# Grouped-query attention decode: K rows of 8 KB in 1 MB loads, two pairs of groups interleaved by halves of the keys

## The chip, the cores and the metric

The kernel runs on one core of one Trainium2 chip. The metric is device time in microseconds (us) of one execution. A core has the matrix engine PE (its weight loads are listed apart, as PEld), the vector engine DVE, the scalar engine ACT, GpSimd (POOL), the queue SP, which in this kernel only issues DMA transfers, and 16 DMA engines that carry them.

## The reference, cut to what matters

```python
B, Hq, Hkv, Sq, Sk, D = 16, 32, 8, 16, 2048, 128      # all bfloat16
k = jnp.repeat(k, Hq // Hkv, axis=1)                  # 4 query heads share one K/V head
v = jnp.repeat(v, Hq // Hkv, axis=1)
scores = jnp.einsum("bhqd,bhkd->bhqk", q, k) * D ** -0.5
p = softmax(scores, axis=-1)
return jnp.einsum("bhqk,bhkd->bhqd", p, v)
```

One group is one (batch, K/V head): 128 groups, each with 64 query rows (4 heads of 16) against 2048 keys. K and V are 512 KB a group, so 134.2 MB of K and V are read once and 4.2 MB of Q and output go beside them.

## The kernel before, in words

Groups are worked in 64 pairs p, the two groups of a pair filling the 128 rows of a tile. For each pair, in the names of the code:

- K: a DMA of 512 KB for each group g into the ring `Kn` (NBK = 10 buffers). Partition a gets the 16 consecutive keys 16a to 16a+15, so each partition receives 4 KB in one piece.
- kx: DVE transposes the tile in 32x32 blocks of 32-bit words into `KT` (L267; NKT = 3 buffers of a pair).
- S: 32 matmuls write the scores into `S_ps` (L340), which fills four PSUM banks and exists once. Each of the four banks holds the keys of 32 partitions of K (a in the code).
- ex: ACT takes the exponential of all 2048 columns in one instruction, into `P` (2 buffers), with the row sums by the accumulator (L278). No maximum is subtracted in this fast program; a second, general program, which does, stands behind a branch at the end and is taken only if a row sum leaves a range.
- pt, pe: 16 PE transposes in two halves into `PT_ps` (L350), each half copied by DVE or ACT to `PT` (L299; NPT = 3).
- V, pv: a DMA of 512 KB for each group into `Vb` (NBV = 14), and 32 matmuls into `O_ps` (L355).
- rc, nm, ST: the reciprocal of the row sum (L284), the scaled copy to `O` (L288 on ACT, L290 on DVE; NBO = 8), and the store of 32 KB.

Q comes in 8 chunks of 256 KB (8 pairs each); POOL rearranges it (qr, L272), PE transposes it (qt, L328) and ACT or DVE copies it out (qe, L299).

Every transfer is issued by SP at L317, in one written order (`dma` in `make_ops`): at step t the two K loads of pair t, the two V loads of pair t - DV (DV = 2) and the store of pair t - DSTORE (DSTORE = 5). SP waits for each transfer's condition before it issues it, so a store that waits for its nm holds back all loads behind it. The order of the work on the other engines is fixed when the kernel is built: `build_schedule` runs a small model of the engines with the durations in `_DUR`, and each engine then follows its list, with semaphore waits taken from `deps`. `HINT` places, for each engine, a mark so many operations ahead of the end for the branch there.

The code that the diff touches follows.

Of the kernel before, what the change touches and what calls it, by code (L numbers as in the profile page):

```python
# [12 lines left out]
NBK = 10  # L13
NBV = 14
# [3 lines left out]
DV = 2  # L18
# [4 lines left out]
HINT = {"pe": 7, "dve": 10, "act": 3, "pool": 1, "sp": 6}  # L23
# [4 lines left out]
    ("dve", "kx"): 1.25, ("dve", "mx"): 2.38, ("dve", "rc"): 0.17, ("dve", "nm"): 0.36,  # L28
    ("dve", "pe"): 0.69, ("act", "pe"): 1.03, ("act", "qe"): 1.06, ("dve", "qe"): 1.25, ("act", "nm"): 0.42,
    ("act", "ex"): 2.22, ("pool", "qr"): 1.6, ("act", "qr"): 1.1, ("dve", "qr"): 1.1,  # L30
# [6 lines left out]
_SIZE = {"K": 0.524, "V": 0.524, "Q": 0.27, "ST": 0.06}  # L37
_ISSUE = 0.5
_T0 = 1.0
_ENGS = {"kx": ("dve",), "mx": ("dve",), "rc": ("dve",), "nm": ("act", "dve"), "pe": ("act", "dve"),  # L40
         "qe": ("act", "dve"), "qr": ("pool",), "ex": ("act",), "qt": ("pe",), "S": ("pe",), "pt": ("pe",), "pv": ("pe",)}
_PRIO = {"S": 0, "mx": 0, "ex": 0, "pt": 1, "pe": 1, "pv": 2, "rc": 2, "nm": 2, "kx": 3, "qr": 3, "qt": 3, "qe": 3}


def make_ops(NP, pairs_per_chunk, general):

    deps = {}
    dma = []
    ch = lambda p: p // pairs_per_chunk
    n_ch = ch(NP - 1) + 1  # L50
    last_of = lambda c: min(NP, (c + 1) * pairs_per_chunk) - 1

    def add(op, *d):
        deps[op] = [x for x in d if x is not None]

    opt = lambda ok, op: op if ok else None
    for c in range(n_ch):
        add(("Q", c), *[opt(c >= 2, ("qr", c - 2, x)) for x in range(4)])
        for x in range(4):
            prev = ("qe", c, x - 1) if x else opt(c >= 1, ("qe", c - 1, 3))  # L60
            add(("qr", c, x), ("Q", c), opt(c >= 1, ("qt", c - 1, x)))
            add(("qt", c, x), ("qr", c, x), prev)
            add(("qe", c, x), ("qt", c, x), opt(c >= 2, ("S", last_of(c - 2))))
    for g in range(2 * NP):
        p = g // 2
        add(("K", g), opt(g >= NBK, ("kx", g - NBK)))
        add(("V", g), opt(g >= NBV, ("pv", (g - NBV) // 2)))
        add(("kx", g), ("K", g), opt(p >= NKT, ("S", p - NKT)))
    for p in range(NP):
        add(("S", p), ("kx", 2 * p), ("kx", 2 * p + 1), *[("qe", ch(p), x) for x in range(4)],  # L70
            opt(p >= 1, ("mx" if general else "ex", p - 1)))
        if general:
            add(("mx", p), ("S", p), opt(p >= 2, ("ex", p - 2)))
        add(("ex", p), ("mx" if general else "S", p), *[opt(p >= 2, ("pt", p - 2, h)) for h in range(2)])
        for h in range(2):
            add(("pt", p, h), ("ex", p), opt(p >= 1, ("pe", p - 1, h)))
            add(("pe", p, h), ("pt", p, h), opt(p >= NPT, ("pv", p - NPT)))
        add(("pv", p), ("pe", p, 0), ("pe", p, 1), ("V", 2 * p), ("V", 2 * p + 1), opt(p >= 1, ("nm", p - 1)))
        add(("rc", p), ("ex", p))
        add(("nm", p), ("pv", p), ("rc", p), opt(p >= NBO, ("ST", p - NBO)))  # L80
        add(("ST", p), ("nm", p))
    qstep = {max(0, c * pairs_per_chunk - QLEAD): c for c in range(n_ch)}
    dma.append(("Q", 0))
    for t in range(NP + max(DV, DSTORE) + 1):
        if t < NP:
            dma += [("K", 2 * t), ("K", 2 * t + 1)]
        if qstep.get(t, 0):
            dma.append(("Q", qstep[t]))
        if 0 <= t - DV < NP:
            dma += [("V", 2 * (t - DV)), ("V", 2 * (t - DV) + 1)]  # L90
        if 0 <= t - DSTORE < NP:
            dma.append(("ST", t - DSTORE))
    return deps, dma


def pair_of(op, pairs_per_chunk):
    if op[0] in ("qr", "qt", "qe"):
        return op[1] * pairs_per_chunk - 1.5
    return op[1] // 2 if op[0] == "kx" else op[1] + {"S": -1.5, "pv": 1.5}.get(op[0], 0)


def build_schedule(NP, pairs_per_chunk, general):

    deps, dma = make_ops(NP, pairs_per_chunk, general)
    left = sorted((op for op in deps if op[0] in _ENGS),
                  key=lambda op: (pair_of(op, pairs_per_chunk), _PRIO[op[0]]))
    done, free = {}, {"pe": _T0, "dve": _T0, "act": _T0, "pool": _T0, "sp": _T0}
    progs = {"pe": [], "dve": [], "act": [], "pool": [], "sp": []}
    dma_left, dma_end = list(dma), _T0 + _DMA_LAT

    def ready(op):
        r = 0.0
        for d in deps[op]:
            if d not in done:
                return None
            r = max(r, done[d])
        return r

    while left or dma_left:
        best = None  # L120
        if dma_left:
            rd = ready(dma_left[0])
            if rd is not None:
                st = max(free["sp"] + _LAT_SAME, rd + _LAT)
                best = ((round(st, 3), -1, -1), st, "sp", dma_left[0])
        seen = 0
        for op in left:
            rd = ready(op)
            if rd is None:
                continue  # L130
            dur = lambda e: _DUR[op[0]] if e == "pe" else _DUR[(e, op[0])]
            engs = ("dve", "act") if op[:2] == ("qr", 0) else _ENGS[op[0]]
            fin = min((max(free[e] + _LAT_SAME, rd + _LAT) + dur(e), e) for e in engs)
            st = fin[0] - dur(fin[1])
            cand = ((round(st, 3), pair_of(op, pairs_per_chunk), _PRIO[op[0]]), st, fin[1], op)
            if best is None or cand[0] < best[0]:
                best = cand
            seen += 1
            if seen > 40:
                break  # L140
        _, st, eng, op = best
        if eng == "sp":
            dma_left.pop(0)
            end = st + _ISSUE
            dma_end = max(dma_end, end + _DMA_LAT) + _SIZE[op[0]] / _BW
            done[op] = dma_end + (_V_LATE if op[0] == "V" else 0.0)
        else:
            left.remove(op)
            end = st + (_DUR[op[0]] if eng == "pe" else _DUR[(eng, op[0])])
            done[op] = end  # L150
        free[eng] = end
        progs[eng].append(op)
    return deps, progs, max(done.values())


def bass_standalone__gqa_softmax__sampling_kernel(
# [28 lines left out]
    Kn = [sb(f"Kn{i}", [128, J * 64], I32) for i in range(NBK)]  # L185
    KT = [sb(f"KT{i}", [128, 2, J * 64], I32) for i in range(NKT)]
    Vb = [sb(f"Vb{i}", [128, J, 128], BF16) for i in range(NBV)]
    Sneg = [sb(f"Sneg{i}", [128, Sk], F32) for i in range(2)]
# [3 lines left out]
    nbias = sb("nbias", [128, NP], F32)  # L192
    rowsum = sb("rowsum", [128, NP], F32)
    ones = sb("ones", [128, 1], F32)
# [13 lines left out]
    rings = {"K": NBK, "V": NBV, "Q": 2, "ST": NBO}  # L208

    class Program:  # L210
        def __init__(self, tag, general):
            self.general = general
            self.deps, self.progs, _ = build_schedule(NP, qch // 128, general)
            self.sem_eng = {e: sem(f"{tag}_{e}") for e in ("pe", "dve", "act", "pool")}
            self.sem_dma = {kind: [sem(f"{tag}_{kind}{i}") for i in range(n)] for kind, n in rings.items()}
            self.where = {op: (e, i + 1) for e in self.sem_eng for i, op in enumerate(self.progs[e])}

        def point(self, op):
            if op[0] in rings:
                n = rings[op[0]]  # L220
                return self.sem_dma[op[0]][op[1] % n], 16 * (op[1] // n + 1)
# [36 lines left out]
    def elementwise(eng, me, prog, before_last=None):  # L258
        waits = prog.waiter(eng, me)
        for op in prog.progs[me]:  # L260
# [5 lines left out]
            if kind == "kx":  # L266
                ins = eng.transpose(KT[(p // 2) % NKT][:, p % 2, :], Kn[p % NBK][:, :])  # L267
# [5 lines left out]
            elif kind == "mx":  # L273
                ins = eng.tensor_scalar(Sneg[p % 2][:, :], S_ps[:, :], -scale, None,
                                        op0=ALU.mult, op1=ALU.min, accum_out=nbias[:, p:p + 1])
            elif kind == "ex":
                src = Sneg[p % 2] if prog.general else S_ps
                ins = eng.activation(  # L278
                    P[p % 2][:, :].rearrange("m (r a j) -> m a r j", a=4, j=32),
                    src[:, :].rearrange("m (a r j) -> m a r j", a=4, j=32), ACT.Exp,  # L280
                    bias=nbias[:, p:p + 1] if prog.general else 0.0, scale=-1.0 if prog.general else scale,
                    accum_out=rowsum[:, p:p + 1])
# [19 lines left out]
    def transfers(sp, prog):  # L302
        waits = prog.waiter(sp, "sp")
        for op in prog.progs["sp"]:
# [3 lines left out]
            s = x % rings[kind]  # L308
            if kind == "K":
                dst, src = Kn[s][:, :].bitcast(BF16), kf[x].rearrange("(a j) d -> a (j d)", j=J)  # L310
            elif kind == "V":
                dst, src = Vb[s][:, :, :], vf[x].rearrange("(a j) d -> a j d", j=J)
# [6 lines left out]
    def matmuls(pe, prog):  # L319
        waits = prog.waiter(pe, "pe")  # L320
        for op in prog.progs["pe"]:
# [11 lines left out]
            elif kind == "S":  # L333
                c, pp = divmod(p, qch // 128)
                for x in range(4):
                    for a in range(4):
                        for gg in range(2):
# [14 lines left out]
            else:  # L352
                for r in range(J):
                    for gg in range(2):
# [3 lines left out]
                            Vb[(2 * p + gg) % NBV][:, r, :],  # L358
# [20 lines left out]
    with nc.Block() as block:  # L379
# [30 lines left out]
        def _(dve):  # L410
            def count_within():
                dve.wait_ge(*fast.point(("ex", NP - 1)))
# [41 lines left out]
```

## Time and profile before

| what | value |
|---|---|
| median of 3 runs | 356.95 us (356.61 to 357.4) |
| the profiled execution, its own time | 355.28 us |
| its span, first to last instruction | 353.4 us |
| granted TensorE clock, mean | 0.971 |
| DMA, share of the span and mean rate | 98.7% of 16 engines, 394 GB/s |
| DVE, PE, ACT busy | 239.4, 233.8, 193.8 us |
| landing of a K load, of a V load (median from issue) | 12.1 us, 13.3 us |

The profile describes one execution. Busy time is given for each engine and as a share of the span; idle time before a group of instructions is put down to whatever released it last. The DMA queues are listed by packets, bytes and the time that the packets took as a share of 16 engines' time; packets on one engine can overlap, so a share may read a little over 100%. Row 2 of the page cuts the span into 40 slices of 8.8 us.

### The profile page before, as it was taken

Reading aid. Unit: us, or ns where it says so; the run is one execution under the profiler, and the core shown is the slowest. Engines: PE = TensorE matmul, PEld = TensorE weight load, DVE = VectorE, ACT = ScalarE, POOL = GpSimd, SP = SyncE. Lnnn points to the kernel's source line nnn. Section 1 sums busy time; section 2 is a strip of 40 time slices with the busy share of each in tenths; the row PEclk is TensorE's granted clock in tenths of the full one; section 3 lists DMA queues with packets and bytes.
Section 4 is the critical chain, followed back from the end, with each engine's and each line's share of the span. In section 5 each row is a group of like instructions: output and inputs, shape, how many; then the busy total and the mean of one; then the engine's idle time right before and its main releaser. Section 6 shows DMA issues by size and latency. Waiting matters only on the chain.

```text
span 353.4 us, 11937 instructions
## 1 busy us (share of the span) xinstructions
PE 233.8 (66%) x5378; PEld 167.9 (48%) x5378; DVE 239.4 (68%) x340; ACT 193.8 (55%) x214; POOL 28.9 (8%) x35
## 2 busy tenths in 40 slices
PE   2499765776666857756556876676656677566663
PEld 1266543554444634544444655454444545444442
DVE  4668786787685666766766676675776647866761
ACT  6458555754347646665456753576554755554450
POOL 1040000300012000310004000040000400000000
PEclk9999999989999998999999988999999989999997
DMA  7999999999999999999999999999999999999971
GB/s 276 414 408 408 413 408 407 412 413 406 413 408 410 412 410 412 408 413 411 410 411 411 408 412 413 395 411 413 409 411 409 406 413 410 403 409 405 411 287 42
DMA packets 47288, 139.24 MB, mean 394 GB/s; under 512 B 13440, under 2 KB 13440, under 8 KB 47232
## 3 DMA queue, kind: packets, MB, share of 16 engines
q1 hardware_dynamic: 47232, 138.43, 98.7%
q8 instruction: 43, 0.70, 0.8%
q14 instruction: 13, 0.11, 0.1%
HBM read 136.31 MB, written 2.10 MB: 392 GB/s over the span
## 4 chain that ended last, share of the span: by engine, by line
DMA 54%; PE 16%; DVE 14%; ACT 7%; SPq 5%; issue 4%
DMA Kn<-in_k_dram 54%; DVE KT L267 8%; ACT P L278 6%; PE S_ps L340 6%; SPq L317 5%; PE PT_ps L350 5%; PE O_ps L355 5%; DVE PT L299 4%; DVE O L290 1%; PE QT_ps L328 1%; ACT O L288 0%; DVE rrec L284 0%; DVE flag L419 0%
## 5 line engine op out<-in xcount | busy, mean ns | idle before, releaser
L267 DVE STREAM_TRANSPOSE KT<-Kn 128x1024 int32<-128x1024 int32 x128 | 158.1, 1238 | 75.7 <-DMA Kn<-in_k_dram 74.6
L278 ACT ACTIVATE P<-S_ps 128x2048 bf16<-128x2048 f32 x64 | 120.1, 1877 | 78.0 <-PE S_ps L340 77.8
L350 PE MATMUL PT_ps<-ident,P 128*128 128x128 bf16 x1024 | 76.0, 225 | 53.9 <-DVE PT L299 38.3
L340 PE MATMUL S_ps<-KT,QT 32*64 32x512 bf16 x2048 | 74.6, 398 | 45.8 <-DVE KT L267 16.8
L350 PEld LDWEIGHTS PT_ps<-ident,P 128*128 128x128 bf16 x1024 | 60.4, 100 | 77.8 <-issue 40.9
L299 DVE COPY PT<-PT_ps 128x1024 bf16<-128x1024 bf16 x102 | 66.1, 672 | 16.7 <-PE PT_ps L350 16.7
L355 PE MATMUL O_ps<-Vb,PT 128*64 128x128 bf16 x2048 | 73.1, 225 | 6.5 <-issue 5.4
L355 PEld LDWEIGHTS O_ps<-Vb,PT 128*64 128x64 bf16 x2048 | 61.8, 113 | 21.2 <-issue 16.9
L340 PEld LDWEIGHTS S_ps<-KT,QT 32*64 32x64 bf16 x2048 | 28.9, 105 | 69.0 <-DVE KT L267 34.3
L272 POOL COPY Qr<-Qn 128x1024 bf16<-128x1024 bf16 x28 | 27.9, 1041 | 250.4 <-DMA Qn<-in_q_dram 250.4
L288 ACT ACTIVATE O<-O_ps,rrec 128x128 bf16<-128x128 f32 x27 | 9.9, 367 | 56.7 <-PE O_ps L355 56.7
L299 ACT ACTIVATE QT<-QT_ps 128x1024 bf16<-128x1024 bf16 x30 | 30.6, 1019 | 6.6 <-PE QT_ps L328 6.6
L299 ACT ACTIVATE PT<-PT_ps 128x1024 bf16<-128x1024 bf16 x26 | 26.6, 1024 | 5.7 <-PE PT_ps L350 5.7
L328 PE MATMUL QT_ps<-ident,Qr 128*128 128x128 bf16 x256 | 22.4, 238 | 8.4 <-ACT Qr L272 4.5
L328 PEld LDWEIGHTS QT_ps<-ident,Qr 128*128 128x128 bf16 x256 | 17.4, 107 | 12.2 <-issue 7.4
L290 DVE TENSOR_SCALAR O<-O_ps,rrec 128x128 bf16<-128x128 f32 x37 | 12.7, 342 | 7.6 <-PE O_ps L355 7.2
L284 DVE RECIPROCAL rrec<-rowsum 128x1 f32<-128x1 f32 x64 | 9.5, 149 | 4.7 <-ACT P L278 3.8
L278 ACT ACTIVATION_READ_ACCUMULATOR P<-S_ps 128x1 f32 x64 | 12.4, 194 | 0.0
L272 DVE COPY Qr<-Qn 128x1024 bf16<-128x1024 bf16 x2 | 1.3, 690 | 3.3 <-DMA Qn<-in_q_dram 3.3
L299 DVE COPY QT<-QT_ps 128x1024 bf16<-128x1024 bf16 x2 | 2.5, 1225 | 1.2 <-PE QT_ps L328 1.1
L272 ACT ACTIVATE Qr<-Qn 128x1024 bf16<-128x1024 bf16 x2 | 2.0, 1049 | 1.3 <-DMA Qn<-in_q_dram 1.3
L272 ACT ACT_TABLE_LOAD x1 | 1.3, 1283 | 0.7 <-PEq L439 0.7
(12 smaller groups left out, 2.2 us busy)
## 6 DMA issues: line engine op xcount, KB each, us to landing
Kn<-in_k_dram SPq DMA_DIRECT2D x128, 512.0 KB, 12.1
Vb<-in_v_dram SPq DMA_DIRECT2D x128, 512.0 KB, 13.3
Qn<-in_q_dram SPq DMA_DIRECT2D x8, 256.0 KB, 12.0
out_dram<-O SPq DMA_DIRECT2D x64, 32.0 KB, 11.0
```

What stands on the lines that cost most here:

```text
L267: ins = eng.transpose(KT[(p // 2) % NKT][:, p % 2, :], Kn[p % NBK][:, :])
L272: ins = eng.activation(dst, src, ACT.Copy) if me == "act" else eng.tensor_copy(dst, src)
L278: ins = eng.activation(P[p % 2][:, :].rearrange("m (r a j) -> m a r j", a=4, j=32), src[:, :].rearrange("m (a r j) -> m a r j", a=4, j=32) ...
L284: ins = eng.reciprocal(rrec[:, p:p + 1], rowsum[:, p:p + 1])
L288: ins = eng.activation(dst, src, ACT.Copy, scale=r)
L290: ins = eng.tensor_scalar(dst, src, r, None, op0=ALU.mult)
L299: ins = eng.activation(dst, src, ACT.Copy) if me == "act" else eng.tensor_copy(dst, src)
L317: sp.dma_start(dst, src).then_inc(prog.sem_dma[kind][s], 16)
L328: ins = pe.transpose(QT_ps[:, 128 * i:128 * (i + 1)], Qr[:, x, i, :], ident[:, :],)
L340: ins = pe.matmul(S_ps[64 * gg:64 * (gg + 1), 512 * a:512 * (a + 1)], QT[c % 2][32 * a:32 * (a + 1), x, 128 * pp + 64 * gg:128 * pp + 64 * ...
L350: ins = pe.transpose(PT_ps[h][:, 128 * t:128 * (t + 1)], P[p % 2][:, 128 * r:128 * (r + 1)], ident[:, :])
L355: ins = pe.matmul(O_ps[64 * gg:64 * (gg + 1), 0:128], PT[p % NPT][:, r, 64 * gg:64 * (gg + 1)], Vb[(2 * p + gg) % NBV][:, r, :], start=(r ...
```

## The change

- K: four groups (two pairs, p = 2s and 2s+1) share the partitions. Load i = 2s + gg is 1 MB and brings group gg of both pairs: 64 partitions hold one group, 64 the other, each partition 32 consecutive keys, 8 KB in one piece. `Kn` has 6 buffers of 1 MB. On the DRAM side the transfer now counts 2 groups, 64 rows, 8 KB; on the side of the chip's memory 128 partitions.
- S: a step u = 2s + h covers one half of the keys (16 of each partition's 32) of both pairs, so `S_ps` holds 1024 columns of either pair. The transposes kx stay as many and as large.
- ex: two instructions of 1024 columns for each pair, with their row sums in `rhalf`, which a new operation rs on DVE adds.
- V: still 512 KB a transfer and 4 KB a partition, but partition 64h + b takes keys 32b + 16h to 32b + 16h + 15, to match K; on the DRAM side the transfer counts 2 halves, 64 rows, 4 KB. The last pair's V comes in two parts (VH), and its pv is cut in two likewise.
- The written order of the transfers: V runs LAG = 5 pairs behind K in place of 2, the store 5 pairs behind V. `Vb` has 7 buffers of a pair (as much memory as before).
- `HINT` is 200, 10000 and 130 for DVE, ACT and SP, and the planner's durations follow the new shapes. In the general program the negated scores use two of the `Kn` buffers.

```diff
-NBK = 10
-NBV = 14
+NBK = 6
+NBK_GENERAL = 4
+NBV = 7
...
-DV = 2
+LAG = 5
...
-HINT = {"pe": 7, "dve": 10, "act": 3, "pool": 1, "sp": 6}
+HINT = {"pe": 7, "dve": 200, "act": 10000, "pool": 1, "sp": 130}
...
-    ("act", "ex"): 2.22, ("pool", "qr"): 1.6, ("act", "qr"): 1.1, ("dve", "qr"): 1.1,
+    ("act", "nm"): 0.42, ("act", "ex"): 1.27, ("pool", "qr"): 1.6, ("act", "qr"): 1.1, ("dve", "qr"): 1.1,
...
+    v_of = lambda p: [("VH", x) for x in halves] if p == NP - 1 else [("V", p)]
...
+    for i in range(NP):
+        add(("K", i), *[opt(i >= nbk, ("kx", 2 * ((i - nbk) // 2) + h, i % 2)) for h in halves])
...
+    for u in range(NP):
+        s, h = divmod(u, 2)
+        for gg in range(2):
+            add(("kx", u, gg), ("K", 2 * s + gg), opt(u >= NKT, ("S", u - NKT)))
+        prev = [("mx" if general else "ex", 2 * ((u - 1) // 2) + pp, (u - 1) % 2) for pp in range(2)] if u else []
+        add(("S", u), ("kx", u, 0), ("kx", u, 1), *[("qe", ch(2 * s), x) for x in range(4)], *prev)
...
+            add(("ex", p, h), ("nb", p) if general else ("S", u), *[opt(p >= 2, ("pt", p - 2, x)) for x in halves])
...
+            add(("pt", p, h), ("ex", p, 0), ("ex", p, 1), opt(p >= 1, ("pe", p - 1, h)))
+            add(("pe", p, h), ("pt", p, h), opt(p >= NPT, ("pv", p - NPT, 0)))
...
+        add(("rs", p), ("ex", p, 0), ("ex", p, 1))
...
-    for t in range(NP + max(DV, DSTORE) + 1):
+    lag = min(LAG, nbk - 1)
+    for t in range(NP + max(lag, DSTORE) + 1):
         if t < NP:
-            dma += [("K", 2 * t), ("K", 2 * t + 1)]
+            dma.append(("K", t))
...
+        if 0 <= t - lag < NP:
+            dma += v_of(t - lag)
+        if 0 <= t - lag - DSTORE < NP:
+            dma.append(("ST", t - lag - DSTORE))
...
-                ins = eng.transpose(KT[(p // 2) % NKT][:, p % 2, :], Kn[p % NBK][:, :])
+                gg, i = op[2], 2 * (p // 2) + op[2]
+                ins = eng.transpose(KT[p % NKT][:, gg, :],
+                                    Kn[i % prog.rings["K"]][:, J * 64 * (p % 2):J * 64 * (p % 2 + 1)])
...
+                    src = S_ps[:, Sk // 2 * (p % 2):Sk // 2 * (p % 2 + 1)]
                 ins = eng.activation(
-                    P[p % 2][:, :].rearrange("m (r a j) -> m a r j", a=4, j=32),
-                    src[:, :].rearrange("m (a r j) -> m a r j", a=4, j=32), ACT.Exp,
+                    P[p % 2][:, :].rearrange("m (r h a j) -> m h a r j", h=2, a=2, j=32)[:, h],
+                    src.rearrange("m (a r j) -> m a r j", a=2, j=32), ACT.Exp,
...
             if kind == "K":
-                dst, src = Kn[s][:, :].bitcast(BF16), kf[x].rearrange("(a j) d -> a (j d)", j=J)
-            elif kind == "V":
-                dst, src = Vb[s][:, :, :], vf[x].rearrange("(a j) d -> a j d", j=J)
+                dst = Kn[s][:, :].bitcast(BF16)
+                src = kf[4 * (x // 2) + x % 2:4 * (x // 2) + x % 2 + 3:2].rearrange("p (b r) d -> p b (r d)", r=2 * J)
+            elif kind[0] == "V":
+                p, part = (x, slice(0, J)) if kind == "V" else (NP - 1, slice(J // 2 * x, J // 2 * (x + 1)))
+                for gg in range(2):
+                    sp.dma_start(
+                        Vb[p % NBV][:, gg, part, :].rearrange("a r d -> a (r d)"),
+                        vf[2 * p + gg].rearrange("(b h r) d -> h b r d", h=2, r=J)[:, :, part, :]
+                        .rearrange("h b r d -> h b (r d)"),
+                    ).then_inc(prog.sem_dma[kind][s], 16)
+                continue
...
                     for a in range(4):
+                        c, pp = divmod(2 * (p // 2) + a // 2, qch // 128)
```

## The prediction

> **What bounds the kernel now.** I read the page first: the shares of the engines, the 40 slices, the DMA queues.
>
> ```profile
> PE 233.8 (66%) x5378; PEld 167.9 (48%) x5378; DVE 239.4 (68%) x340; ACT 193.8 (55%) x214; POOL 28.9 (8%) x35
> ...
> DMA  7999999999999999999999999999999999999971
> GB/s 276 414 408 408 413 408 407 412 413 406 413 408 410 412 410 412 408 413 411 410 411 411 408 412 413 395 411 413 409 411 409 406 413 410 403 409 405 411 287 42
> DMA packets 47288, 139.24 MB, mean 394 GB/s; under 512 B 13440, under 2 KB 13440, under 8 KB 47232
> ...
> q1 hardware_dynamic: 47232, 138.43, 98.7%
> ```
>
> No compute engine passes 68%, while the DMA engines are full in 37 slices of 40 at 395 to 414 GB/s. The kernel is a stream of 139 MB with a short head and a tail. The longest wait, POOL for Q, costs nothing: POOL has 29 us of work.
>
> Two views tell whether compute could become the limit. In the groups by line:
>
> ```profile
> L267 DVE STREAM_TRANSPOSE KT<-Kn 128x1024 int32<-128x1024 int32 x128 | 158.1, 1238 | 75.7 <-DMA Kn<-in_k_dram 74.6
> L278 ACT ACTIVATE P<-S_ps 128x2048 bf16<-128x2048 f32 x64 | 120.1, 1877 | 78.0 <-PE S_ps L340 77.8
> ```
>
> DVE, the busiest engine, waits 74.6 us for K itself: compute keeps up and is paced by the loads. The chain of waits says the same (54% of it is K's loads).
>
> Last the end: windows of the DMA and the timeline.
>
> ```profile
> 338.00:340.00 2.00, 0.82 (x36) 0.61 (x38) 1.75 (x4) 1.54 (x2) 0.00 (x0) 1.00 0.92 364
> 340.00:341.00 1.00, 1.00 (x37) 0.46 (x22) 0.16 (x1) 0.11 (x1) 0.00 (x0) 1.00 0.79 311
> 341.00:345.00 4.00, 2.89 (x63) 2.45 (x60) 2.74 (x5) 1.86 (x2) 0.00 (x0) 1.00 0.54 212
> 345.00:346.00 1.00, 0.46 (x17) 0.49 (x19) 0.35 (x1) 0.00 (x0) 0.00 (x0) 1.00 0.31 104
> ...
> 345.51 0.95 PEld L355 LDWEIGHTS O_ps<-Vb,PT 128*64 128x64 bf16 x32 [0.67 <-issue]
> 345.54 1.08 PE L355 MATMUL O_ps<-Vb,PT 128*64 128x128 bf16 x32 [0.54 <-DVE O L290]
> ...
> 347.16 1.08 PE L355 MATMUL O_ps<-Vb,PT 128*64 128x128 bf16 x32 [0.54 <-DVE O L290]
> ...
> 348.28 0.35 DVE L290 TENSOR_SCALAR O<-O_ps,rrec 128x128 bf16<-128x128 f32 x1 [0.99 <-PE O_ps L355]
> ```
>
> The last two columns of the windows are DMA share and GB/s. From 341 to 345 half the engines' time is used at half the rate: I read it as half of the engines having finished some 4 to 5 us before the rest. The last V has landed by about 345.7. The last two pv then wait for the nm before them (DVE O), so a compute chain ends the kernel: last scaled copy done at 348.63, store, 353.4.
>
> **The change part by part.** I sum against the profiled execution: span 353.4, its own time 355.28. The median of runs, 356.95, lies 1.67 above that; I add it at the end.
>
> K's packets. K has 128 loads of 128 rows of 4 KB, 16384 packets; after, 64 loads of 128 rows of 8 KB, 8192. Of the 13440 short packets 64 x 128 = 8192 are output rows of 256 B; the other 5248 are 16 for each of 328 transfers, its completion marks. After there are 64 K, 130 V, 8 Q and 64 store transfers, 266 x 16 = 4256 marks. VH adds 256 packets of 2 KB. So 8192 + 992 - 256 = 8928 packets fewer, 558 for each engine. Fixed cost of a packet: no less than 0, if time goes by bytes. Upper end from the last store alone (window 348.5 to 351.2):
>
> ```profile
> q1 hardware_dynamic: 144, 0.03, 5.6%
> ```
>
> 5.6% of 16 x 2.7 us is 2.42 us; 144 packets hold 128 x 256 B, 1.28 us at 25.7 B/ns (411 GB/s over 16); 1.14 us / 144 = 8 ns. The gain lies between 0 and 558 x 8 ns = 4.5 us. A 4 KB load is neither end, so I take 4 ns: -2.2 us, all on the path, as the stream is full.
>
> [...]
>
> The end. With V 5 pairs behind K, the last K lands some 6 MB before the last V, 15 us at 411 GB/s. Its transposes, S, exponentials and PE transposes took from 335.08 to 344.9 before, 10 us, so they lie under V's loads. What is left behind the last V: half a pv (16 matmuls, 0.55 us by 1.08 for 32), nm 0.35 with 0.15 of handoffs, and the way from 348.63 to 353.4, 4.8 us: 5.9 us, against 353.4 - 345.7 = 7.7 now: -1.8. Bounds: -2.5, if V's landing is half a microsecond later than I read; 0, if the last pv still queues behind earlier ones.
>
> The dips. Slices of 395, 403, 403 and 405 cost 38/411 x 8.8 = 0.8 us. SP's queue waits 126 us for nm to send stores (64.8 ACT O, 61.3 DVE O), and loads stand behind. After, with V 5 behind and the store 5 behind V, five V and five K of 1 MB are out when SP waits, 25 us of work against a landing of 12 to 13 now. A stall of nm (7.1 us at most) is covered: -0.5 (bounds 0 and -0.8). Without that cover each microsecond that SP waits beyond the queue's content is lost.
>
> What beside the stream gets longer. ACT: 128 exponentials of 1024 columns. The nearest rows are copies of 128x1024, 1019 to 1024 ns, plus 194 to read the accumulator: 1.22 us. Bounds of the instruction: 0.94, half of 1877, and 1.88, no gain from halving. 128 x 1.22 = 156 against 64 x 2.07 = 132.5: +23 us, ACT 217 (62%). DVE: 64 additions at most like the reciprocal, 149 ns: +9.5, DVE 249 (71%); behind each wait only reciprocal and nm, due 10 us later. Kx, S, pt and pv keep number and size. These hide under 5.3 us a pair (139.24 MB / 64 / 411).
>
> The loop to watch is `S_ps`, which exists once. Now S to next S is 3.3 us (exponentials at 337.57 and 340.89 with one S between). After, a half-step of two pairs is S 1.13, two exponentials 2.44, handoffs 0.13: two half-steps 7.4 us for two pairs, for which the stream needs 10.6. The rest of ACT's work, 193.8 - 132.5 = 61 us, adds 1.9 for two pairs if none of it lies under S: 9.3. Covered, with 1.3 to spare.
>
> V's rows are as many and as long but 8 KB apart in turn; the trace has only V read in order. No gain; at worst all V runs at the poorest slice, 395 against 411: 4% of 170 us, +7. I take 0, as the two halves together read the same contiguous 512 KB. The head: the first S stood at 13.3 behind Q's copies, and 2 MB of K had landed by 11: 0 (to +1). `HINT`: its effect lies in the 4.8 us at the end; 0, bounds -1 and +2.
>
> Sum: -2.2 - 1.8 - 0.5 = -4.5. Span 348.9, own time 350.8, as a median 352.4.
>
> **The rivals.** (a) Nothing measurable (within 0.2%, 0.7 us, what a measurement can tell from no change): rows of 8 KB cost per byte what 4 KB does, and the last pv still queues behind pv(62). The half-idle DMA from 341 to 345 speaks for a limit that packet size doesn't touch; the DVE O waits speak against. 356.95 less at most 0.7: 356.6.
>
> (b) Slower, the ring of `S_ps`: it decides once two half-steps pass 10.6 us, that is when an exponential with its accumulator costs over (10.6 - 2.26 - 0.26 - 1.9) / 4 = 1.55 us. At the upper bound, 1.88 + 0.19, two pairs take 12.7 us, 32 x 12.7 + 13 + 10 = 429; slightly over the point, 11 us: 375. The copies of 128x1024 at 1020 ns speak against, and DVE could take more of ACT's copies.
>
> (c) Slower, a transfer that is spread over fewer engines. All transfers now count 128 rows outermost on both sides, and the 16 marks for each show all 16 engines. K and V after count 2 outermost in DRAM. If that count sets the spread, 134.2 MB go over two engines of 25.7 GB/s: 2610 us, and the marks of a load fall from 16 to 2. No row shows a transfer with a small outer count, for or against; an even spread by the 128 partitions would give the forecast.
>
> [...]
>
> (d) Slower by V's interleaved reads: 1 to 2% over, 357.7 to 362.
>
> **How the numbers follow.** Forecast 0.66 (it takes in the packet gain or the shorter end failing alone: 354.7, 354.2), (a) 0.07, (b) 0.08, (c) 0.12, (d) 0.07. Low end: all bounds at their best, -4.5 - 2.5 - 0.8 - 1 = -8.8: 348.2; I take 347.5. High end: into (d), 359.5; (b), (c) and a rest of (d) stay out, near 0.2. The forecast's own range is 348 to 356. Faster by over 0.2%: 0.66; within: 0.07; slower: 0.27.
>
> **What would show it.** q1 with some 38300 packets, 12450 of them under 512 B; slices at 412 to 416 and none under 408; ACT near 217, DVE near 249; exponentials of about 1020 ns; the chain's end on V's landing, with 16 matmuls, nm and store behind; the last kx over 10 us ahead of it. It is wrong if slices stay at 410, if DVE or ACT stop waiting for loads, or if the DMA share falls to an eighth.

## The result and the profile after

The changed kernel takes 2561.8 us (2561.5 to 2562.1, 4 runs) against 357.2 us before: 7.174 times as long, 95% interval 7.162 to 7.186. The forecast was 352.4 us with a range of 347.5 to 359.5; the time lies near rival (c), a transfer spread over fewer engines, which had been priced at 2610 us and given 0.12.

The profiled execution took 2562.1 us, with a span of 2560.2. The page of the changed kernel, shares of the engines, granted clock, slices and queues:

```profile
PE 377.4 (15%) x5378; PEld 266.8 (10%) x5378; DVE 225.2 (9%) x365; ACT 230.7 (9%) x381; POOL 29.0 (1%) x35
...
PEclk9755555555555555555555555555555555555555
DMA  1111111111111111111111111111111111111111
GB/s 58 53 53 53 53 57 54 54 54 54 58 54 54 54 54 57 54 54 54 54 57 54 54 54 54 57 54 53 54 54 58 54 54 54 54 54 54 54 54 53
DMA packets 35642, 139.21 MB, mean 54 GB/s; under 512 B 9732, under 2 KB 9732, under 8 KB 27396
...
q1 hardware_dynamic: 35588, 138.42, 13.3%
```

In all 40 slices, now of 64 us, the DMA engines are busy for about one eighth of their time and move 53 to 58 GB/s, where it had been 395 to 414. The bytes are the same 138.4 MB. 13.3% of 16 engines is 2.1 engines: two that never rest, and a little on the others. The packet records of the trace (start, length and size of every packet) say so directly: at least two packets are under way in 99.7% of the span, three or more in 4.6%. A 4 KB packet takes 159 ns (median) in both kernels. So the two engines are no slower than before; there are only two of them.

The short packets say which transfers use so few engines. 9732 packets are under 512 B; 8192 of them are output rows. The other 1540 are completion marks: 16 for each of the 8 Q loads and 64 stores make 1152, and 388 remain for the 64 K loads and 130 V loads, exactly 2 each. Before there were 16 for every transfer.

The waits of the changed kernel, the longest first (us in total, times, longest):

```profile
DVE KT L287 <- DMA Kn<-in_k_dram: 2210.5, 64, 37.5
POOL Qr L293 <- DMA Qn<-in_q_dram: 1933.3, 7, 316.1
ACT O L318 <- PE O_ps L394: 1154.6, 47, 36.2
PEld O_ps L394 <- DMA Vb<-in_v_dram: 1043.9, 64, 35.2
```

DVE waited 74.6 us for K before, now 2210.5. No compute engine is the limit: each is idle for five sixths of the span or more. SP's queue in the timeline (start, duration, number of transfers):

```profile
1000.38 8.02 SPq L355 DMA_DIRECT2D Kn<-in_k_dram  x1
...
1008.45 27.90 SPq L345 DMA_DIRECT2D Vb<-in_v_dram  x2
```

To hand over two V loads takes SP 27.9 us, where the median of one was 0.48 us. What holds SP in that time is not shown.

Two groups of the page belong to steps of the prediction:

```profile
L306 ACT ACTIVATE P<-S_ps 128x1024 bf16<-128x1024 f32 x128 | 130.4, 1021 | 699.2 <-PE S_ps L378 658.8
...
L378 PE MATMUL S_ps<-KT,QT 32*64 32x512 bf16 x2048 | 115.4, 588 | 529.9 <-DVE rowsum L312 306.2
```

The halved exponential takes 1021 ns (estimate 1.02 us). A score matmul averages 588 ns where it was 398; the mean granted clock fell with it, from 0.971 to 0.546 of full speed.

### The profile page after: what moved, and what is told of

It is laid out like the page before. It is cut to its first block, busy times and chain, and to the rows that moved or that the text cites. A ratio compares the mean times of both kernels' runs of the same rounds, so it can differ in the third digit from the quotient of the medians.

```text
span 2560.2 us, 12003 instructions
## 1 busy us (share of the span) xinstructions
PE 377.4 (15%) x5378; PEld 266.8 (10%) x5378; DVE 225.2 (9%) x365; ACT 230.7 (9%) x381; POOL 29.0 (1%) x35
## 2 busy tenths in 40 slices
DMA packets 35642, 139.21 MB, mean 54 GB/s; under 512 B 9732, under 2 KB 9732, under 8 KB 27396
## 3 DMA queue, kind: packets, MB, share of 16 engines
q1 hardware_dynamic: 35588, 138.42, 13.3%
## 4 chain that ended last, share of the span: by engine, by line
DMA 55%; SPq 37%; PE 3%; DVE 3%; issue 1%; ACT 1%; another core or an unknown queue 1%; POOL 0%
DMA Kn<-in_k_dram 50%; SPq L345 23%; SPq L355 13%; DMA Vb<-in_v_dram 4%; DVE KT L287 2%; PE S_ps L378 2%; DMA Qn<-in_q_dram 1%; PE PT_ps L388 1%; DVE PT L329 0%; ACT P L306 0%; PE QT_ps L366 0%; PE O_ps L394 0%; DVE QT L329 0%; ACT PT L329 0%
## 5 line engine op out<-in xcount | busy, mean ns | idle before, releaser
L287 DVE STREAM_TRANSPOSE KT<-Kn 128x1024 int32<-128x1024 int32 x128 | 154.4, 1229 | 2210.5 <-DMA Kn<-in_k_dram 2210.5
L394 PE MATMUL O_ps<-Vb,PT 128*64 128x128 bf16 x2048 | 122.9, 314 | 1032.4 <-DMA Vb<-in_v_dram 1032.4
L394 PEld LDWEIGHTS O_ps<-Vb,PT 128*64 128x64 bf16 x2048 | 107.3, 172 | 1052.6 <-DMA Vb<-in_v_dram 1043.9
L388 PE MATMUL PT_ps<-ident,P 128*128 128x128 bf16 x1024 | 116.6, 303 | 535.1 <-DVE PT L329 512.8
L378 PE MATMUL S_ps<-KT,QT 32*64 32x512 bf16 x2048 | 115.4, 588 | 529.9 <-DVE rowsum L312 306.2
L306 ACT ACTIVATE P<-S_ps 128x1024 bf16<-128x1024 f32 x128 | 130.4, 1021 | 699.2 <-PE S_ps L378 658.8
L388 PEld LDWEIGHTS PT_ps<-ident,P 128*128 128x128 bf16 x1024 | 101.0, 141 | 575.1 <-issue 475.6
L329 ACT ACTIVATE PT<-PT_ps 128x1024 bf16<-128x1024 bf16 x50 | 50.8, 1016 | 140.5 <-PE O_ps L394 103.2
L329 DVE COPY PT<-PT_ps 128x1024 bf16<-128x1024 bf16 x78 | 50.6, 662 | 1.3 <-PE PT_ps L388 1.3
L329 ACT ACTIVATE QT<-QT_ps 128x1024 bf16<-128x1024 bf16 x25 | 25.5, 1021 | 270.4 <-PE QT_ps L366 270.4
L293 POOL COPY Qr<-Qn 128x1024 bf16<-128x1024 bf16 x28 | 27.9, 1040 | 1933.3 <-DMA Qn<-in_q_dram 1933.3
L306 ACT ACTIVATION_READ_ACCUMULATOR P<-S_ps 128x1 f32 x128 | 25.2, 197 | 0.0
L312 DVE TENSOR_TENSOR rowsum<-rhalf 128x1 f32<-128x1 f32 x64 | 9.0, 171 | 1.9 <-ACT P L306 1.9
```

The source lines that it names most:

```text
L287: ins = eng.transpose(KT[p % NKT][:, gg, :], Kn[i % prog.rings["K"]][:, J * 64 * (p % 2):J * 64 * (p % 2 + 1)])
L293: ins = eng.activation(dst, src, ACT.Copy) if me == "act" else eng.tensor_copy(dst, src)
L306: ins = eng.activation(P[p % 2][:, :].rearrange("m (r h a j) -> m h a r j", h=2, a=2, j=32)[:, h], src.rearrange("m (a r j) -> m a r j", a ...
L312: ins = eng.tensor_tensor(rowsum[:, p:p + 1], rhalf[:, p, 0:1], rhalf[:, p, 1:2], op=ALU.add)
L329: ins = eng.activation(dst, src, ACT.Copy) if me == "act" else eng.tensor_copy(dst, src)
L378: ins = pe.matmul(S_ps[64 * gg:64 * (gg + 1), 512 * a:512 * (a + 1)], QT[c % 2][32 * a:32 * (a + 1), x, 128 * pp + 64 * gg:128 * pp + 64 * ...
```

## The experiments

The time of before in the three groups of runs was 356.47 us (e1 to e4), 356.02 (e5 to e8) and 356.16 (e9 to e12); each run is compared with its own.

**e1_outer4: an outermost count of 4, and nothing else.**

```diff
-                dst, src = Kn[s][:, :].bitcast(BF16), kf[x].rearrange("(a j) d -> a (j d)", j=J)
+                dst, src = Kn[s][:, :].bitcast(BF16), kf[x].rearrange("(b c j) d -> c b (j d)", c=4, j=J)
...
-                dst, src = Vb[s][:, :, :], vf[x].rearrange("(a j) d -> a j d", j=J)
+                dst = Vb[s][:, :, :].rearrange("a j d -> a (j d)")
+                src = vf[x].rearrange("(b c j) d -> c b (j d)", c=4, j=J)
```

> The kernel before, with one edit: the rows of K and of V are dealt to the partitions in 4 blocks, so that every K and V load counts 4 outermost in DRAM (4 blocks, 32 rows, 4 KB) against 128 partitions. Bytes, transfers, order and computation are those of before. Theory (the outermost count sets how many engines carry a load): in the changed kernel two engines moved 134.7 MB (all K and V, an eighth of Q and stores) in 2558 us, 26.3 GB/s each; four engines then need 135.2 MB / 105.3 GB/s = 1284 us, so 1290 us in all, with 256 x 4 + 72 x 16 = 2176 completion marks and 10368 packets under 512 B. Rival (the loss lies in the dealt rows or in loads of 1 MB, and all 16 engines are used): under 450 us here, with 13440 short packets as before.

Measured: 1308.0 us. The queues of its page:

```profile
DMA packets 44215, 139.22 MB, mean 107 GB/s; under 512 B 10368, under 2 KB 10368, under 8 KB 44160
...
q1 hardware_dynamic: 44160, 138.42, 26.4%
```

10368 short packets, to the packet; 26.4% of 16 engines is 4.2 engines. The time is 1.4% over the expectation. By the packet records at least four packets are under way in 98.8% of the span, five or more in 11.6%. A count of 4 gave four engines, in the kernel before with its 512 KB loads and 4 KB rows.

**e9_before_outer2: the same edit with c=2.**

> The kernel before, with K's and V's rows dealt to the partitions in 2 blocks, so that each load counts 2 outermost in DRAM; nothing else of the change (no 8 KB rows, no 1 MB loads, no halves, no lag). Theory: this alone gives the changed kernel's time: 134.7 MB over two engines of 26.3 GB/s, 2560 us, within 1% of 2562; 8192 + 256 x 2 + 72 x 16 = 9856 short packets. Rival (half of the changed kernel's loss comes from its other parts): under 2300.

Measured: 2583.4 us, 0.8% over the changed kernel.

```profile
DMA packets 43704, 139.23 MB, mean 54 GB/s; under 512 B 9856, under 2 KB 9856, under 8 KB 43648
...
q1 hardware_dynamic: 43648, 138.42, 13.3%
```

9856 short packets, as worked out. This one edit of the source patterns alone gives the whole of the changed kernel's loss; the changed kernel, with its fewer and longer rows, is 22 us shorter than this one.

**e3_k_in_halves: K alone mended** (the semaphore counts, left out here, follow).

```diff
-                dst = Kn[s][:, :].bitcast(BF16)
-                src = kf[4 * (x // 2) + x % 2:4 * (x // 2) + x % 2 + 3:2].rearrange("p (b r) d -> p b (r d)", r=2 * J)
+                for y in range(2):
+                    sp.dma_start(
+                        Kn[s][64 * y:64 * (y + 1), :].bitcast(BF16),
+                        kf[4 * (x // 2) + x % 2 + 2 * y].rearrange("(b r) d -> b (r d)", r=2 * J),
+                    ).then_inc(prog.sem_dma[kind][s], 16)
+                continue
```

> The changed kernel, each K load of 1 MB issued as two of 512 KB, one for each half of the partitions (64 rows of 8 KB outermost on both sides, same addresses). V is left as it is. Theory: K now uses all 16 engines, V stays on two, which carry 67.1 MB of V, an eighth of K (8.4 MB) and of the rest (0.5 MB): 76.0 MB / 52.7 GB/s = 1443 us. Rival (loads of 8 KB rows or the deep queue are slow whatever the engines): above 1900 us.

Measured: 1664.2 us, 15% over the theory's number and under the rival's. Between its first slice and its last three the rate swings between 71 and 97 GB/s. SP waits 332 us for exponentials, but the two engines of V hardly stood still for it: by the packet records at least two packets are under way in 99.4% of the span. The sum went wrong in the packets' length. An 8 KB packet of K takes 607 ns on average, where it took 311 in the changed kernel, and a 4 KB packet 183 in place of 160; an estimate from these times is some 150 us more for K's share on each engine and 180 for V's, enough for the 221 us over the sum. The next runs show the same of loads into half of the partitions.

**e4_all_in_halves: K and V mended in the same way** (V as four loads of 64 rows for a pair).

> The changed kernel with both K and V issued by halves of the partitions (K two loads of 512 KB, V four of 256 KB for a pair; 64 rows outermost on both sides). Addresses, layout, order and computation are those of the changed kernel. Theory: all loads on 16 engines, 8192 + 16 x (128 + 260 + 72) = 15552 short packets, and the forecast's own sum applies but for the marks, which now are more than before and not fewer: 351 to 355 us. Rival (the S_ps ring or the lag of 5 is a second cause): 360 us and up, with ACT or DVE no longer waiting for loads.

Measured: 550 to 563 us in six runs, 1.552 times before (1.546 to 1.557). The theory's number failed, and the rival's reason as well: ACT and DVE have 228 and 224 us of work, and DVE waits 297 us for K. The DMA is full and slow:

```profile
DMA  8999999999999999999999999999999999999992
GB/s 195 215 225 224 231 238 255 275 258 264 279 271 257 269 272 252 263 270 259 268 251 256 257 267 254 250 259 265 267 260 247 260 261 253 254 264 271 274 268 75
DMA packets 41464, 139.25 MB, mean 251 GB/s; under 512 B 15552, under 2 KB 15552, under 8 KB 33216
```

All marks are there (15552 short packets), so all 16 engines work, at 251 GB/s on average. Their packets take longer: 264 ns (median) for 4 KB in place of 159, 527 for 8 KB in place of 309. So 16 engines alone did not give the rate of before, 394 GB/s on average.

**e7_before_halves and e8_before_columns: the kernel before, each load cut in two**, by partitions and by columns (V's lines and the semaphore counts are left out here).

```diff
-                dst, src = Kn[s][:, :].bitcast(BF16), kf[x].rearrange("(a j) d -> a (j d)", j=J)
+                for y in range(2):                                       # e7; V likewise
+                    sp.dma_start(Kn[s][64 * y:64 * (y + 1), :].bitcast(BF16),
+                                 kf[x].rearrange("(a j) d -> a (j d)", j=J)[64 * y:64 * (y + 1), :]).then_inc(prog.sem_dma[kind][s], 16)
+                for y in range(2):                                       # e8; V likewise
+                    sp.dma_start(Kn[s][:, 512 * y:512 * (y + 1)].bitcast(BF16),
+                                 kf[x].rearrange("(a j) d -> a (j d)", j=J)[:, 1024 * y:1024 * (y + 1)]).then_inc(prog.sem_dma[kind][s], 16)
```

> The kernel before, each K and V load of 512 KB issued as two of 256 KB, one for partitions 0 to 63, one for 64 to 127; rows of 4 KB, natural order, all else as before. Theory (a transfer into half of the partitions does not reach the full rate, although 64 rows divide over 16 engines): the 251 GB/s of e4_all_in_halves, 139.2 MB / 251 = 555 us; 480 to 580. Rival (e4 lost its time to V's rows read 8 KB apart, or to the S_ps ring): 358 to 370 here, as nothing but the number of transfers differs from before.

> The kernel before, each K and V load of 512 KB issued as two of 256 KB over all 128 partitions, 2 KB of each partition's row: as many transfers and as large as in e7_before_halves, but each reaches every partition. Theory of half partitions: no such loss; 2304 packets more an engine at 4 ns are 9 us: 357 to 376. Rival (smaller transfers are what costs): as slow as e7.

Measured: e7 476.3 us, e8 373.7 us. The same number of transfers of the same size; only the one that reaches half of the partitions loses its rate. The slices of e7:

```profile
GB/s 204 234 231 234 244 244 249 249 247 253 248 251 250 248 241 258 266 282 315 290 357 376 387 285 352 393 392 302 326 359 347 315 286 344 369 375 367 362 341 70
```

The rate stays at 204 to 258 for 16 slices of 40, then climbs, and swings up to 393. So the same transfers run slowly first and near the full rate later; what changes between is not shown. e8 is 17.7 us over before with 2304 packets more for an engine: 7.7 ns each.

**e2_outer16: 16 engines, rows dealt in 16 blocks** (the edit of e1 with c=16).

> The same edit with 16 blocks of 8 rows: neighbouring partitions read rows 64 KB apart from each other in turn, and the outermost count is 16. Theory: all 16 engines, 13440 short packets, and the time of before within 1% (355 to 361). Rival (the dealt rows themselves are slow to read): clearly slower than before, 380 us and up, as no dealing goes further than this one.

Measured: 445.8 us in the fastest of four runs (the others 454 to 495), with all 13440 short packets. That is 1.25 times before, so the theory's second half failed: with 16 engines the time of before does not return. The number fits the rival, slow reading of dealt rows, as well; e10 and e11 test that. The slices begin as in e7:

```profile
GB/s 201 239 235 239 244 249 252 253 259 280 306 334 383 297 386 386 376 320 318 359 375 389 279 395 387 366 289 306 368 376 371 254 358 390 342 343 367 362 274 35
```

**e10_k_columns and e11_k_outer16: which of the two, far reads or the outermost count.** Both start from e5_adjacent_groups below and load K in two transfers of 512 KB (the semaphore counts are left out here).

```diff
-                src = kf[2 * x:2 * x + 2].rearrange("g (b r) d -> (g b) (r d)", r=2 * J)
+                for y in range(2):       # e10; e11 reads "g (e y w r) d -> y (g e) w (r d)", y=2, w=8
+                    sp.dma_start(Kn[s][:, J * 64 * y:J * 64 * (y + 1)].bitcast(BF16),
+                                 kf[2 * x:2 * x + 2].rearrange("g (b y r) d -> y (g b) (r d)", y=2, r=J)[y]).then_inc(prog.sem_dma[kind][s], 16)
```

> The kernel of e5_adjacent_groups with each K load of 1 MB issued as two of 512 KB, one for the first and one for the second 4 KB of every partition's 8 KB: 128 rows of 4 KB, 8 KB apart in DRAM, the reading that V had in the changed kernel, now with 128 outermost. If interleaved reading costs nothing: e6_adjacent_4kb (4 KB packets) plus 64 completion marks an engine at 7 ns, 0.5 us: about 1.3 us under before. If it costs what the prediction's bound for it allowed (4% on this half of the stream): 7 us over that, 5 us slower than before.

> The kernel of e10_k_columns, but each of the two K loads takes 16 blocks of 8 neighbouring rows of 4 KB, the blocks 64 KB apart: outermost count 16 against 128, all 16 engines, same bytes, packets and marks as e10. (K's keys then stand in another order than V's rows: that part of the computation is changed, the work is not.) It asks what slowed e2_outer16 and e7_before_halves, whose rates began near 240 GB/s and climbed towards 390. Theory W (an outermost count of 16 hands every engine 8 neighbouring partitions, and several engines write to the same part of the memory at once, until they drift apart): K at 240 to 300 GB/s, 390 to 450 us in all, again climbing with time. Theory R (reading rows 64 KB apart was slow in e2): the rows here are neighbours, so equal to e10 within 3 us.

Measured: e10 355.2 us, 0.997 times before (0.996 to 0.998): rows read 8 KB apart cost nothing that shows. e11 570.3 us, with K alone changed and neighbouring rows:

```profile
GB/s 214 242 279 248 247 260 258 256 252 253 247 253 252 247 254 250 248 253 251 237 237 230 235 236 236 233 242 246 242 253 244 256 261 255 252 260 254 244 325 58
DMA packets 48600, 139.25 MB, mean 245 GB/s; under 512 B 14496, under 2 KB 14496, under 8 KB 48544
```

The rows that e11 reads together are neighbours, so theory R falls. Theory W's numbers fail too: 570 us is well over its 390 to 450, the rate stays near 250 to the end, and the climb that it expected did not come, so the part about drifting apart is not shown. What is shown: with 16 engines, 128 partitions and the same packets, an outermost count of 16 in place of 128 for K's loads takes the rate of the whole stream from 410 to 250 GB/s.

The packet records say how the rate is lost. In these runs 15 to 17 packets of 4 KB or more are under way for four fifths of the time, as in before, but in all except e10 each takes longer. The median of a 4 KB packet in ns, in the first and in the last tenth of the span:

| run | first | last |
|---|---|---|
| before, and e10 | 159 | 159 |
| e2 | 279 | 181 |
| e4 | 292 | 239 |
| e7 | 287 | 171 |
| e11 | 271 | 241 |

Why they take longer is not shown: the reason that theory W gives was the author's guess, and no run shows which engine writes where. The order of reading fits less well: e2's blocks lie 4 KB apart with rows 64 KB apart, e11's blocks 64 KB apart with rows next to each other, and both begin near 240 GB/s. No run varies the distance in DRAM with the outermost count kept at 16.

**e5_adjacent_groups: the change without its outermost count of 2.** The pairs are chosen so that K's two groups are neighbours in DRAM. (Left out here: the semaphore counts, the output's two stores, and the columns of Q, which follow the new pairs.)

```diff
-                    P[p % 2][:, :].rearrange("m (r h a j) -> m h a r j", h=2, a=2, j=32)[:, h],
+                    P[p % 2][:, :].rearrange("m (r a j h) -> m h a r j", h=2, a=2, j=32)[:, h],
...
-                src = kf[4 * (x // 2) + x % 2:4 * (x // 2) + x % 2 + 3:2].rearrange("p (b r) d -> p b (r d)", r=2 * J)
+                src = kf[2 * x:2 * x + 2].rearrange("g (b r) d -> (g b) (r d)", r=2 * J)
...
-                        vf[2 * p + gg].rearrange("(b h r) d -> h b r d", h=2, r=J)[:, :, part, :]
-                        .rearrange("h b r d -> h b (r d)"),
+                        vf[4 * (p // 2) + 2 * gg + p % 2].rearrange("(a r) d -> a r d", r=J)[:, part, :]
+                        .rearrange("a r d -> a (r d)"),
```

> The changed kernel with other pairs: pair 2s is made of groups 4s and 4s+2, pair 2s+1 of 4s+1 and 4s+3. A 1 MB load of K then brings two neighbouring groups, one contiguous piece of DRAM, and counts 128 rows of 8 KB outermost on both sides; V is loaded in natural order, 128 rows of 4 KB (the exponential writes P in the matching order), and a pair's output goes out in two stores of 64 rows. Lag, buffers, S by halves, half exponentials and hints are those of the changed kernel. Theory (the outermost count was the one cause; the forecast's sum is right for the rest): 39330 packets, 7900 fewer than before, 494 an engine at 4 ns = 2.0 us, and 1.8 for the end and 0.5 for the dips: 4.3 us under the 356.5 of before, 352.2. Rival 1 (a second cause: the S_ps ring, or the lag): 360 and up. Rival 2 (nothing to gain from 8 KB rows and a later V): within 1 us of before.

Measured: 350.6 us, 0.984 times before (0.982 to 0.986): faster than both kernels. Its page:

```profile
span 348.8 us, 12067 instructions
...
DMA  8999999999999999999999999999999999999971
GB/s 313 423 414 411 416 410 414 415 415 413 414 416 414 416 416 414 415 414 419 413 417 415 413 412 416 411 417 415 413 416 412 413 419 414 412 418 412 380 297 50
DMA packets 39383, 139.24 MB, mean 399 GB/s; under 512 B 13472, under 2 KB 13472, under 8 KB 31136
...
q1 hardware_dynamic: 39328, 138.43, 98.3%
...
L287 DVE STREAM_TRANSPOSE KT<-Kn 128x1024 int32<-128x1024 int32 x128 | 154.4, 1228 | 97.8 <-DMA Kn<-in_k_dram 86.7
L306 ACT ACTIVATE P<-S_ps 128x1024 bf16<-128x1024 f32 x128 | 164.9, 1307 | 39.9 <-PE S_ps L382 33.0
```

39328 packets in q1 as worked out; most slices at 411 to 419. DVE still waits 86.7 us for K, so compute is not the limit, though ACT is busy for 255.4 us: the exponential, now writing every other element of P, takes 1307 ns in place of 1021. The end of its chain of waits (start, us, what):

```profile
332.17 11.03 DMA Vb<-in_v_dram
343.19 0.04 issue
343.24 0.66 PE O_ps L398 x16
343.89 0.02 issue
343.92 0.35 DVE O L320
344.27 0.05 DVE flag L462
```

It ends on the last V, half a pv, nm and the store, as the prediction drew it.

**e6_adjacent_4kb: e5 with K's rows in 4 KB packets** (`max_dma_last_dim=4096` at `sp.dma_start`).

> The kernel of e5_adjacent_groups with K's rows of 8 KB cut into two pieces of 4 KB (same transfers, same addresses, 8192 packets more, 512 an engine). If a packet costs 4 ns as the forecast took it: 2.0 us above e5. At its upper bound of 8 ns: 4.1 us above. If time goes by bytes: equal to e5 within 0.5 us.

Measured: 354.3 us, 0.995 times before (0.993 to 0.997), 3.7 us over e5. 3.7 us / 512 = 7.2 ns a packet. This is the price that the forecast took as 4, between 0 and 8. The slices are back at 400 to 413.

**e12_before_lag4: the lag alone, in the kernel before.**

```diff
-DV = 2
+DV = 4
...
-DSTORE = 5
+DSTORE = 9
```

> The kernel before with V 4 pairs behind K in place of 2 and the store 5 behind V (the deepest lag its 10 K buffers allow); nothing else. The forecast's terms for the end and the dips alone: 1.8 + 0.5 = 2.3 us faster, the last K's chain under V's loads, but with a whole pv (0.55 us more than half a one) behind the last V: 1.7 us faster, 0.8 to 2.5. If the last pv still queue behind one another as before: within 0.5 us of before.

Measured: 356.2 us, 1.000 times before (0.999 to 1.002): nothing. The end of its chain:

```profile
334.19 12.61 DMA Vb<-in_v_dram
346.80 0.25 issue
347.05 1.10 PE O_ps L355 x32
348.15 0.02 issue
348.17 0.35 DVE O L290
```

The chain has the predicted form, but V lands at 346.8. The trace of before, asked for the V loads issued after 336 us, has the landing there too:

```profile
L317 SPq DMA_DIRECT2D Vb<-in_v_dram x2: 342/387/432, 336.3 to 336.7; - x2
...
DMA to landing us min/median/max: 9.5/9.9/10.3
```

The last V load is issued at 336.7 and lands 10.3 us later, at 347.0; the 345.7 of the prediction is about where the load before it lands (336.3 + 9.5). So the last pv, at 347.16, waited for its V as long as for the nm before it, and the lag brings V only 0.2 us forward.

## Why the prediction was wrong

**The step that failed** is one that the forecast's sum never wrote as a term: all K and V transfers were taken to run on 16 engines after the change, as before, and the other case was set at 0.12 as rival (c). The reasoning stopped at "no row shows a transfer with a small outer count, for or against" and kept the present rate for it. The rows did show that every transfer of before counted 128 outermost; the change alters exactly that number, so the rate of the old rows was no evidence for the new transfers, and the chance of 0.12 was an estimate with no row behind it. The marks then came out to the packet: 2 a load here, as rival (c) had it, and 4 in e1. What the runs showed in the step's place: two engines, at 53 to 58 GB/s together in place of 395 to 414, which cost some 2205 us over before, where the sum had nothing. e9 gives this loss by the outermost count alone, and e5 takes it away with that count.

Rival (c) had the right mechanism and the right sign (marks falling from 16 to 2), and its price of 2610 us came from 25.7 GB/s an engine. Two engines that never rest move 134.7 MB, which is all of K and V and an eighth of the rest, in some 2560 us: 26.3 GB/s each.

**What the rest of the sum was worth** is seen in e5, where that one thing is taken away: -5.4 us measured, -4.3 expected of it. That the two lie close is partly luck, as the terms show.

- Packets: mechanism right, the term too small. 494 packets an engine at 7.2 ns are 3.6 us in place of 2.0. The trace of before held a better price in its packet records: a 2 KB packet takes 84 ns and a 4 KB one 159, so two short ones cost 9 ns of their own time more than one long one.
- The end: form right, size wrong. V lands at 347.0 and not at 345.7, so 6.4 us stood behind it and not 7.7, and the lag alone gains nothing (e12). In e5 V lands at 343.2, 3.8 us sooner, of which the packets are 3.6, and 5.6 us stand behind it. The 0.8 us between 6.4 and 5.6 are half a pv (0.66 against 1.10 us), a handoff (0.05 against 0.14) and the way from the last nm to the end (4.5 against 4.8). That last part is no gain that is shown: with the `HINT` of before it took 5.5 us in e12. Together this is 4.6 us, the difference of the two spans (353.4 and 348.8); of the other 0.8, 0.7 is the distance from the profiled execution of before (355.28) to the median beside e5 (356.02).
- The dips: in e12 SP waits 22 us for nm where it had waited 126, and nothing is gained. The term of 0.5 us is not confirmed.
- ACT and DVE: the exponential was right (1021 ns for 1.02 us), but the totals were not: 230.7 us for 217, and 225.2 for 249. The planner moved copies of `PT` from DVE to ACT (50 on ACT where there were 26). Neither reached the path.
- Rival (b), the `S_ps` ring: absent, even at 1307 ns an exponential, which lies under its point of 1.55 us with the accumulator's 0.19.
- Rival (d): absent by e10, which reads K as V was read here. Rival (a) falls with e5: the gain is 5.4 us.

## What to carry to other kernels

Before a DMA's pattern is changed for longer rows, write down the outermost count of both sides, and treat a transfer whose count the trace has never shown as unpriced: here a count of 2 in DRAM took the DMA share from 98.7 to 13.3% of 16 engines while partitions, bytes and rows all looked better. After the first run, divide the completion marks by the transfers; here that told in one line how many engines carried each load: 2 marks where the share was 2.1 engines, 4 where it was 4.2 (e1). Cutting such a load into half-partition pieces, or raising the count to 16, brought back 16 marks a load but only 251 (e4) and 245 GB/s (e11); choosing other data so that 128 rows stand outermost brought back the rate too, 399 GB/s on average (e5), and then 8 KB rows were worth 1% (e5 against e6).

## What was not expected of the hardware

- Sixteen engines alone did not give the full rate: transfers of 64 partitions ran at 251 GB/s (e4) and 293 (e7, mean), K loads of outermost count 16 at 245 in all (e11), against 394 before. The engines were not idle: their packets took up to 1.8 times as long. In e2 and e7 the rate of one execution climbed from about 240 to 390 GB/s and then swung below that.
- A packet of a load costs 7.2 ns besides its bytes (e6 against e5), and 7.7 by e8 against before.
- With loads on two engines, the hand-over of two V loads held SP for 27.9 us, where one took 0.48 us before.
- With PE busy for 15% of the span its granted clock was 0.5 in 38 of 40 slices, and the mean of a score matmul rose from 398 to 588 ns. The matmul times of a kernel that waits for loads were no guide to those of the full one.
